# A filter by FFT followed by soft mixture of experts: the softmax chain's steps in another order along the pairs, and the first transform unit of batch 1 behind the first pair

## The chip, the cores and the metric

The kernel runs on one core of a Trainium2 chip. TensorE (PE in the rows) multiplies matrices, VectorE (DVE), ScalarE (ACT) and GpSimd (POOL) work on tiles, and SyncE (SP) issues most DMAs. The metric is device time in microseconds, the median of several executions of the same program; smaller is better.

## The reference

Eight sequences of 2496 rows and 256 channels are filtered in the frequency domain, and the result goes through a soft mixture of 8 experts with 4 slots each. The softmax over the rows (`d`) runs over all 19968 rows of all batches; the one over the slots (`c`) is local to a row.

```python
X = np.fft.rfft(x, axis=1)                      # x: 8 x 2496 x 256
y = np.fft.irfft(X * (filt_r + 1j * filt_i)[None], n=2496, axis=1)
x = y.reshape(19968, 256)
logits = x @ phi                                # 32 slots
d = np.exp(logits - logits.max(0)); d /= d.sum(0) + 1e-09
slot_input = (d.T @ x).reshape(8, 4, 256)
slot_out[e] = np.maximum(slot_input[e] @ w1[e], 0.0) @ w2[e]
c = np.exp(logits - logits.max(1)); c /= c.sum(1) + 1e-09
out = c @ slot_out
```

## The kernel before

**Stages.** A sequence of 2496 rows is transformed in two stages, each a set of small matrix products. Batch 0 is transformed from x directly: `first_stage`, then `turn(c)` transposes a stripe on PE and copies it out (L483, L486). Batches 1 to 7 go in units (b, u), u from 0 to 5: x is loaded, `fold_x` makes sums and differences `sd` and `eo` on DVE and POOL (L378), `s1_unit` multiplies on PE (s, L406), ACT copies the product to `at` (L422), and that goes to DRAM (`a_dram`) and comes back transposed as `ash`. Names such as `s1_1_0` are batch and unit.

**Pairs.** Every batch has five pairs. `x_pair` does the second stage on PE (x, L503) and multiplies by the filter on DVE (t2 at L528, x at L530, the sums y at L531 and L532; from batch 6 the last of them is on POOL). `t_pair` transposes y (PE, L541) and copies it (`yt`, ACT, L547), and `l_unit` makes logits against phi (PE l, L558) and copies them (`lt`, ACT, L569). `x_4_3` is x of batch 4, pair 3. The main loop runs over 80 slots, two to a pair, and a slot also emits the s1 units due in it (`slot_of`).

**Chain.** The batches are grouped as (0,1), (2,3), (4,5), (6,), (7,). Behind each group a generator `chain(g)` brings the logits into the order of time and joins the group to a running softmax: ltr, v1, v, lg (logits; the column maxima `cm` and `cmax` on DVE), mt (transposed maxima, `mx`), mb (spread over partitions, `m_run`), d (DVE L702 subtracts, ACT L710 takes exp), then u, u2 and dd (the inverse steps on PE), z and s (PE sums against y, folded into `s_run` on DVE with the factor `al`, L776 to L781), and `rows()`, the other softmax, in two halves (`rm`, a subtraction, exp, `r_all`). A chain runs while the next batch's pairs run: `hop_slot` takes as many steps of it in slot n as the list `PACE` says. After that the order is a scheduler's, from the order of writing, priorities and the marks `not_before` and `behind`. An engine executes its instructions in that order, so one that waits holds up all behind it.

**End.** The last two chains and the experts' products run after the pairs (about 283 to 331 us), and then the output is formed and written until the end.

Of the kernel before, what the change touches and what calls it, by code (L numbers as in the profile page):

```python
# [86 lines left out]


# [195 lines left out]
def fft_soft_moe(ctx, tc, x0, w0, x, ff, phi, wx, cst, w1q, out):  # L284
# [75 lines left out]
    def fold_x(b, u):  # L360

        lo, hi = PIECE[u]
        w = (hi - lo) * P
        xs = xts.pop((b, u)).rearrange("q k a d -> q (k a d)")[:, 0 : 4 * w].rearrange("q (k a d) -> q k a d", k=2, a=2)
        sd = proda.tile([P, 4 * DIM], F32, tag="sd", name=f"sd{b}_{u}", bufs=DB)
        eo = proda.tile([P, 4 * DIM], F32, tag="eo", name=f"eo{b}_{u}", bufs=EB)
        sd, eo = (
            t[:, 0 : 4 * w].rearrange("q (f a d) -> q f a d", f=2, a=2) for t in (sd, eo)
        )
        early = (b, u) < (1, 2)  # L370
        for k, (o, i0, i1, op) in enumerate((
            (sd[:, 0], xs[:, 0], xs[:, 1], ALU.add),
            (sd[:, 1], xs[:, 0], xs[:, 1], ALU.subtract),
            (eo[:, 0], sd[:, :, 0], sd[:, :, 1], ALU.add),
            (eo[:, 1], sd[:, ::-1, 0], sd[:, ::-1, 1], ALU.subtract),
        )):
# [80 lines left out]
    def first_stage(u):  # L457

        lo, hi = PIECE[u]
        for h in range(lo, hi):  # L460
# [8 lines left out]
            for i in range(2):  # L469
                k = 2 * PK * h + PK * i  # L470
                j = min(PK, N2 - k)
                held[h % 2 + 3] = copy(a0_t[:, :, :, k : k + j], ps[:, i, :, 0:j].rearrange("q g j t -> q t g j"))

    def turn(c):

        if c % 2 == 0:
            ashs[0, c // 2] = prod.tile([P, 4, DIM], F32, tag="ash", name=f"ash0_{c}", bufs=NA)
        ash = ashs[0, c // 2][:, c % 2 * 2 : c % 2 * 2 + 2]
        pt = ps_c.tile([P, 2, 2, P], F32, tag="c", name=f"turn_{c}")
        for k in range(2):  # L480
            for dh in range(2):
                g = a0_t[:, 2 * c + k, 2 * dh : 2 * dh + 2].rearrange("q c k -> q (c k)")
                ins = pe.transpose(pt[:, k, dh, :], g, ident)  # L483
                if c < 2:
                    behind("pe", ins)
        ins = (dve.tensor_copy if c == 1 else act.copy)(ash, pt.rearrange("k p h d -> k p (h d)"))  # L486
        if c == 1:
            held[4] = ins

    def x_pair(b, i):  # L490

# [35 lines left out]
            ys[b, 2 * i + c] = y[:, :, c]  # L527
        dve.tensor_tensor(out=t2, in0=ps[:, ::-1], in1=fiv, op=ALU.mult)  # L528
        add, part = (pool_e, y) if b >= PA else (dve, ps)
        dve.tensor_tensor(out=part, in0=ps, in1=frv, op=ALU.mult)  # L530
        dve.tensor_tensor(out=y[:, 1], in0=part[:, 1], in1=t2[:, 1], op=ALU.add)  # L531
        added[0] = add.tensor_tensor(out=y[:, 0], in0=part[:, 0], in1=t2[:, 0], op=ALU.subtract)  # L532

    def t_pair(b, i):
# [59 lines left out]
    def chain(g):  # L594
# [84 lines left out]
        with tc.high_priority():  # L679
# [72 lines left out]
        for t0 in range(0, HT, TG):  # L752
# [12 lines left out]
            if t0 != 0:  # L765
                yield "dd"

        pz = psum([P, 1], f"z_{g}")
        for b2 in range(nb):
            for j in range(4):  # L770
# [37 lines left out]
        def rows():
            rm = (const if late else wk).tile([KR, NX], F32, tag=f"rm{max(g, NG - 3)}", name=f"rm_{g}", bufs=1)
            rs = r_all[:, g, 0:NX]  # L810
            step = NX // 2
            for x0 in range(0, NX, step):
                sl = slice(x0, x0 + step)
                ins = dve.tensor_reduce(out=rm[:, sl], in_=lgf[:, sl], axis=AX.X, op=ALU.max)
                if x0 == 0 and "sit" in queue:
                    behind("sit", ins)
                if not late:
                    not_before(ins, ended[1])
                    not_before(ins, added[0])
                rmb = rm[:, sl].rearrange("s (x o) -> s x o", o=1).broadcast_to([KR, step, SLOTS])  # L820
                dve.tensor_tensor(out=lgf[:, sl], in0=lgf[:, sl], in1=rmb, op=ALU.subtract)
                ins = act.activation(lgf[:, sl], lgf[:, sl], AF.Exp)
                if not late:
                    not_before(ins, ended[0])
                yield "rows"
                dve.tensor_reduce(out=rs[:, sl], in_=lgf[:, sl], axis=AX.X, op=ALU.add)
                yield "rows"
            dve.tensor_scalar(out=rs, in0=rs, scalar1=1e-9, scalar2=None, op0=ALU.add)
            dve.reciprocal(out=rs, in_=rs)
            if g < NSPILL:  # L830
                c_dram[g] = scr.tile([KR, NH, 2, nb, SLOTS], F32, name=f"c_dram{g}", bufs=1)
                for lo, hi in ((0, CR), (CR, KR)):
                    sp.dma_start(c_dram[g][lo:hi], lg_t[lo:hi])
# [82 lines left out]
    def hop(k=0):  # L916
        if 0 <= k < len(active):
            try:
# [308 lines left out]
```

## Time and profile before

| | us |
|---|---|
| median of the runs (387.44 to 388.2) | 387.52 |
| the profiled execution | 388.1 |
| its span | 386.2 |
| PE busy in it | 332.2 (86%) |
| DVE busy | 277.8 (72%) |
| ACT busy | 190.4 (49%) |
| POOL busy | 181.9 (47%) |

A row of the trace gives the start and the length of a group of like instructions, then engine, line, operation and tiles; the bracket at its end is how long the engine had been idle before it and what released it. Matmul rows count passes, so a number behind x on PE is not a count of lines in the program. PEclk is the share of full clock granted to TensorE, 1.00 being 2.4 GHz and 0.50 being 1.2 GHz.

### The profile page before, as it was taken

What the parts mean: (1) busy time and instruction counts of PE and PEld (TensorE: products, weight loads), DVE (VectorE), ACT (ScalarE), POOL (GpSimd) and SP (SyncE); (2) the same over time, 40 slices, a digit from 0 to 9 for tenths busy, and PEclk for the clock granted to TensorE, in tenths of its full rate; (3) what the DMA queues carried; (4) which work ended last, traced back from release to release, by engine and by line L of the source; (5) the groups of instructions that cost most, each with busy time, mean ns of one, the idle gap of its engine ahead of it and who ended that gap; (6) DMA issues with size and microseconds to landing.
All of it is one profiled execution on the core that took longest, in us unless ns stands there. A gap on an engine that the chain in (4) does not pass through costs nothing.

```text
span 386.2 us, 10001 instructions
## 1 busy us (share of the span) xinstructions
PE 332.2 (86%) x4054; PEld 201.7 (52%) x4054; DVE 277.8 (72%) x406; ACT 190.4 (49%) x393; POOL 181.9 (47%) x178
## 2 busy tenths in 40 slices
PE   8877898889987996987899789799979999989860
PEld 7732343445344543633555444466657635878750
DVE  2489799997896689779928975882976462688540
ACT  2663555546564444662554556365245421676430
POOL 0068978987677465868428581320311302560000
PEclk9999999999998999999699999999989999999655
DMA  8998899899798278979745875951895785499997
GB/s 303 399 378 250 247 279 329 283 341 387 229 319 260 86 208 288 351 204 289 233 122 137 236 215 146 336 161 56 305 347 223 269 290 129 176 415 414 416 415 289
DMA packets 42013, 103.88 MB, mean 269 GB/s; under 512 B 4252, under 2 KB 22556, under 8 KB 39792
## 3 DMA queue, kind: packets, MB, share of 16 engines
q1 hardware_dynamic: 41278, 102.89, 77.8%
q8 instruction: 32, 0.52, 0.5%
q10 hardware_dynamic: 690, 0.36, 0.3%
q14 instruction: 13, 0.11, 0.1%
HBM read 63.11 MB, written 40.12 MB: 267 GB/s over the span
## 4 chain that ended last, share of the span: by engine, by line
PE 52%; DVE 18%; DMA 12%; ACT 7%; issue 4%; POOL 1%; ACTq 0%; DVEq 0%; SPq 0%
PE x L503 8%; PE t L541 7%; PE s L406 7%; DMA out<-ob 5%; PE s L592 5%; ACT at L422 4%; DVE t L528 4%; PE v L592 4%; DMA ff_t<-in_ff 4%; PE u L592 3%; DVE x L530 3%; PE l L558 3%; PE dd L592 3%; DVE d L702 2%; PE out L1177 2%
## 5 line engine op out<-in xcount | busy, mean ns | idle before, releaser
L378 POOL TENSOR_TENSOR eo<-sd 128x512 f32<-128x512 f32 (+1 forms) x80 | 102.2, 1299 | 78.9 <-DVE sd L378 39.2
L528 DVE TENSOR_TENSOR t<-x,ff_t 128x1024 f32<-128x1024 f32 x40 | 48.6, 1215 | 34.2 <-PE x L503 31.9
L547 ACT COPY yt<-t 128x512 f32<-128x512 f32 x80 | 43.6, 588 | 59.9 <-PE t L541 59.8
L503 PE MATMUL x<-ash,cst_t 64*64 64x512 f32 (+3 forms) x352 | 48.9, 583 | 10.0 <-ACT at L422 8.6
L422 ACT COPY at<-s 128x1024 f32<-128x1024 f32 (+1 forms) x42 | 39.5, 941 | 21.4 <-PE s L406 12.9
L406 PE MATMUL s<-eo,w1q_t 64*64 64x512 f32 (+1 forms) x336 | 43.4, 587 | 4.5 <-ACT at L422 4.5
L378 POOL TENSOR_TENSOR sd<-xt 128x512 f32<-128x512 f32 (+1 forms) x36 | 43.9, 1224 | 2.4
L530 DVE TENSOR_TENSOR x<-x,ff_t 128x1024 f32<-128x1024 f32 x30 | 37.0, 1233 | 2.9
L541 PEld LDWEIGHTS t<-cst_t,y 128*128 128x128 f32 x232 | 25.0, 141 | 26.6 <-DVE y L532 10.1
L541 PE MATMUL t<-cst_t,y 128*128 128x128 f32 x232 | 32.8, 280 | 7.0 <-DVE y L532 5.0
L378 DVE TENSOR_TENSOR sd<-xt 128x512 f32<-128x512 f32 (+1 forms) x48 | 37.9, 815 | 0.0
L558 PE MATMUL l<-yt,phi_t 128*32 128x128 f32 x640 | 31.8, 287 | 7.0 <-ACT yt L547 6.8
L1177 PE MATMUL out<-so,st 32*128 32x256 f32 x468 | 35.1, 328 | 2.4 <-ACT ob L1182 1.3
L1177 PEld LDWEIGHTS out<-so,st 32*128 32x128 f32 x468 | 30.1, 214 | 6.7 <-ACT ob L1182 3.5
L532 POOL TENSOR_TENSOR y<-y,t 128x512 f32<-128x512 f32 x9 | 15.0, 1665 | 36.6 <-DVE y L530 31.4
L1182 DVE COPY ob<-out 128x512 f32<-128x512 f32 (+1 forms) x40 | 25.0, 670 | 8.5 <-DMA out<-ob 6.5
L558 PEld LDWEIGHTS l<-yt,phi_t 128*32 128x32 f32 x640 | 17.7, 112 | 22.2 <-ACT yt L547 16.5
L1182 ACT COPY ob<-out 128x512 f32<-128x512 f32 (+1 forms) x40 | 21.7, 582 | 14.8 <-DMA out<-ob 9.0
L503 PEld LDWEIGHTS x<-ash,cst_t 64*64 64x64 f32 (+1 forms) x352 | 12.7, 133 | 24.4 <-ACT at L422 15.3
L592 PE MATMUL s<-y,dd 128*32 128x256 f32 x232 | 19.8, 381 | 0.0
L592 PEld LDWEIGHTS u<-cst_t,d 117*64 117x64 f32 (+3 forms) x440 | 14.9, 139 | 7.0 <-ACT yt L547 2.3
L592 PE MATMUL v<-cst_t,lsb 128*64 128x66 f32 (+1 forms) x400 | 17.4, 235 | 0.0
(127 smaller groups left out, 512.4 us busy)
## 6 DMA issues: line engine op xcount, KB each, us to landing
xt<-in_x SPq DMA_DIRECT2D x35, 512.0 KB
ash<-a_dram SPq DMA_DIRECT2D x35, 512.0 KB
out<-ob SPq DMA_DIRECT2D x17, 1024.0 KB
a_dram<-at SPq DMA_DIRECT2D x70, 240.0 KB
w<-in_wx SPq DMA_DIRECT2D x22, 512.0 KB
x_t<-in_x SPq DMA_DIRECT2D x5, 512.0 KB
ff_t<-in_ff SPq DMA_DIRECT2D x10, 256.0 KB
ff_t<-in_wx SPq DMA_DIRECT2D x5, 512.0 KB
```

What stands on the lines that cost most here:

```text
L378: ins = eng.tensor_tensor(out=o, in0=i0, in1=i1, op=op)
L406: ins = pe.matmul(bf[64 * c : 64 * c + 64, r], w1q_t[q, c], eo[q, c].rearrange("q f d -> q (f d)"), start=True, stop=True,)
L422: copied[0] = act.copy(av, bf.rearrange("q r (f d) -> q f r d", f=2))
L503: ins = pe.matmul(ps[64 * k : 64 * k + 64, r, lo:hi], w[rows], ash[rows, lo:hi, k], start=True, stop=True)
L528: dve.tensor_tensor(out=t2, in0=ps[:, ::-1], in1=fiv, op=ALU.mult)
L530: dve.tensor_tensor(out=part, in0=ps, in1=frv, op=ALU.mult)
L541: ins = pe.transpose(pt[:, dh, r, :], ys[b, 2 * i + c][:, r, dh * P : (dh + 1) * P], ident)
L547: copied[0] = act.copy(yt[:, c], pt)
L558: ins = pe.matmul(pl[32 * j : 32 * j + 32], phi_t[:, dh, :], yt[:, j // 2, dh, :, N2 * (j % 2) : N2 * (j % 2) + N2], start=(dh == 0), stop ...
L592: line(pe.matmul(*a, **k))
L1177: nc.tensor.matmul(prs[k][:, mm, :], sts[n][q, hs, c0 : c0 + P], so[q, ho], start=(i == 0), stop=(i == 2))
L1182: copy(ob[:, nm * k : nm * (k + 1), :], prs[k])
```

## The change

It has four parts.

1. Unit (1,0)'s s1 moves from ahead of the loop into slot 0, behind `x_pair(0, 0)`; the copy of stripe 1 moves from DVE to ACT; and the DVE share of `eo` is kept to unit (1,0) alone.
2. The list `PACE` becomes `PACES`, one list per group. The steps lg4/lg8, mt and mb are drawn into the code of one x pair (`urge`), and the marks order them within its DVE work; u, u2, dd and what follows come earlier in the pairs.
3. `rows()` is a generator of its own, put in the list `side` once dd is done, and advanced in slots in which the chain takes no step.
4. The list of the third group (batches 4 and 5) has no empty slots behind the maxima, so its z and s come earlier too.

```diff
-PACE = (3, 3, 3, 0, 1, 1, 0, 0, 0, 4, 4, 5, 0, 0)
+PACES = ((3, 3, 2, 1, 0, 1, 0, 2, 2, 2, 2) + 4 * (1, 0) + (2,),) * 2 + ((3, 3, 2, 1, 0, 1, 0, 2, 2, 2, 2, 2, 2, 2),)
...
     if b == 1:
-        return u - 1
+        return max(u - 1, 0)
...
-        early = (b, u) < (1, 2)
+        early = (b, u) == (1, 0)
...
-        ins = (dve.tensor_copy if c == 1 else act.copy)(ash, pt.rearrange("k p h d -> k p (h d)"))
+        ins = act.copy(ash, pt.rearrange("k p h d -> k p (h d)"))
         if c == 1:
-            held[4] = ins
+            turned[0] = ins
...
-        dve.tensor_tensor(out=part, in0=ps, in1=frv, op=ALU.mult)
-        dve.tensor_tensor(out=y[:, 1], in0=part[:, 1], in1=t2[:, 1], op=ALU.add)
+        spread = urge("lg8")
+        if spread:
+            held[5] = marks["pe"]
+        ins = dve.tensor_tensor(out=part, in0=ps, in1=frv, op=ALU.mult)
+        if spread:
+            not_before(ins, marks["mx"])
+            urge("mt")
+        ins = dve.tensor_tensor(out=y[:, 1], in0=part[:, 1], in1=t2[:, 1], op=ALU.add)
+        if spread:
+            not_before(ins, marks["m"])
...
-            dve.tensor_reduce(out=mx, in_=pm, axis=AX.X, op=ALU.max)
+            marks["mx"] = dve.tensor_reduce(out=mx, in_=pm, axis=AX.X, op=ALU.max)
...
+        if not late:
+            yield "mb"
...
+        if not late:
+            side.append(rows())
         pz = psum([P, 1], f"z_{g}")
...
-        if g < NG - 2:
-            yield from rows()
-        else:
+        if late:
             late_rows.append(rows())
...
-    for b, u in units[1:]:
+    for b, u in units:
...
     fold_x(1, 0)
-    s1_unit(1, 0)
     sign_tables(0)
...
+    def urge(mark):
+        if active and active[0][0] < NG - 2 and at_mark.get(active[0][0]) == mark:
+            hop()
+            return True
+        return False
...
-        for _ in range(next(steps[active[0][0]], HOPS if active[0][0] == NG - 3 else 1) if paced else HOPS):
+        count = next(steps[active[0][0]], HOPS) if paced else HOPS
+        for _ in range(count):
             if active and active[0][0] < NG - 2:
                 hop()
+        if side and (not paced or count == 0):
+            if next(side[0], None) is None:
+                side.pop(0)
```

**The start, on PE.** Before, the instructions behind stripe 1's turn stand so (`turn_c` is the transposition of stripe c, `s1_1_0` the product of unit (1,0), `x_0_0` the first pair of batch 0; its further pieces are left out of the list by what follows here):

```order
L483 MATMUL turn_2_304<-cst_t_73,a0_t_122 128x128 x4
L483 MATMUL turn_3_328<-cst_t_73,a0_t_122 128x128 x4
L483 MATMUL turn_4_364<-cst_t_73,a0_t_122 128x128 x4
L483 MATMUL turn_5_401<-cst_t_73,a0_t_122 128x128 x4
L483 MATMUL turn_6_440<-cst_t_73,a0_t_122 128x128 x4
L406 MATMUL s1_1_0_244<-eo1_0_238,w1q_t_72 64x256 x4
L483 MATMUL turn_7_478<-cst_t_73,a0_t_122 128x128 x4
L503 MATMUL x_0_0_281<-ash0_0_224,cst_t_73 64x256 x2
```

Now the same engine and place:

```order
L505 MATMUL x_0_0_269<-ash0_0_224,cst_t_73 64x256
L485 MATMUL turn_2_292<-cst_t_73,a0_t_122 128x128 x4
L505 MATMUL x_0_0_269<-ash0_0_224,cst_t_73 64x256
L505 MATMUL x_0_0_269<-ash0_0_224,cst_t_73 64x512
L505 MATMUL x_0_0_269<-ash0_0_224,cst_t_73 64x256 x2
L505 MATMUL x_0_0_269<-ash0_0_224,cst_t_73 64x512
L485 MATMUL turn_3_328<-cst_t_73,a0_t_122 128x128 x4
L406 MATMUL s1_1_0_299<-eo1_0_238,w1q_t_72 64x256 x4
```

The first pair has moved ahead of five turns and of `s1_1_0`.

**The second group's maxima and d, on DVE.** Before, from the last column maximum to `al` (t2, x and the two yb rows are one pair; sd is a unit's fold):

```order
L677 TENSOR_REDUCE cmax_77<-cm_1_1922 117x32
L528 TENSOR_TENSOR t2_4_3_2048<-x_4_3_2043,ff_t_101 128x1024
L530 TENSOR_TENSOR x_4_3_2043<-x_4_3_2043,ff_t_101 128x1024
L531 TENSOR_TENSOR yb_4_2_1982<-x_4_3_2043,t2_4_3_2048 128x512
L532 TENSOR_TENSOR yb_4_2_1982<-x_4_3_2043,t2_4_3_2048 128x512
L378 TENSOR_TENSOR sd6_3_2089<-xt6_3_1797 128x512
L684 TENSOR_REDUCE mx_1_2037<-mt_1_2035 32x1
L528 TENSOR_TENSOR t2_4_4_2110<-x_4_4_2105,ff_t_101 128x1024
L530 TENSOR_TENSOR x_4_4_2105<-x_4_4_2105,ff_t_101 128x1024
L531 TENSOR_TENSOR yb_4_2_1982<-x_4_4_2105,t2_4_4_2110 128x512
L532 TENSOR_TENSOR yb_4_2_1982<-x_4_4_2105,t2_4_4_2110 128x512
L378 TENSOR_TENSOR sd6_4_2141<-xt6_4_1862 128x512
```

(`m_run1`, the three instructions of `d_1` and `al_1` follow there.) Now:

```order
L690 TENSOR_REDUCE cmax_77<-cm_1_1917 117x32
L697 TENSOR_REDUCE mx_1_2048<-mt_1_2046 32x1
L535 TENSOR_TENSOR x_4_3_2039<-x_4_3_2039,ff_t_101 128x1024
L703 TENSOR_TENSOR m_run1_79<-mb_1_2051,m_run0_78 128x32
L539 TENSOR_TENSOR yb_4_2_1968<-x_4_3_2039,t2_4_3_2044 128x512
L542 TENSOR_TENSOR yb_4_2_1968<-x_4_3_2039,t2_4_3_2044 128x512
L378 TENSOR_TENSOR sd6_3_2089<-xt6_3_1792 128x512
L717 TENSOR_TENSOR d_1_2076<-lg_1_1916,m_run1_79 117x512 x2
L717 TENSOR_TENSOR d_1_2076<-lg_1_1916,m_run1_79 117x384
L820 TENSOR_TENSOR al_1_2352<-m_run0_78,m_run1_79 128x32
```

The maxima and `m_run` stand within pair 4_3, d ahead of pair 4_4 instead of behind it; the first and the third group have the same order (the first has no `al`).

**The same place on ACT.** Before:

```order
L547 COPY yt_4_3_2115<-t_4_3_1_2122 128x512
L422 COPY at6_2_2133<-s1_6_2_2128 128x1024
L569 COPY lt_4_1941<-l_4_3_2147 128x128
L547 COPY yt_4_4_2169<-t_4_4_0_2170 128x512
L777 ACTIVATE al_1_2352<-al_1_2352 128x32
```

and now:

```order
L557 COPY yt_4_3_2115<-t_4_3_1_2122 128x512
L821 ACTIVATE al_1_2352<-al_1_2352 128x32
L422 COPY at6_2_2133<-s1_6_2_2128 128x1024
L725 ACTIVATE d_1_2076<-d_1_2076 117x512 x2
```

The exponential of `al_1`, which reads what DVE makes behind `d_1`, has moved ahead of the copy `at6_2`.

In the third group's z and s on PE, all eight z products and 32 of the 40 terms of `s_2` stand ahead of `x_7_2` now; before, all of them stood behind it.

## Rows read from the trace of the kernel before

**Rows 1.** The chain of waits by engine, shares of the span (page, part 4).

```profile
PE 52%; DVE 18%; DMA 12%; ACT 7%; issue 4%; POOL 1%; ACTq 0%; DVEq 0%; SPq 0%
```

**Rows 2.** Windows: length, busy time (instructions) of PE, PEld, DVE, ACT, POOL; PEclk; DMA.

```profile
16.70:32.00 15.30, 12.10 (x84) 6.28 (x83) 13.99 (x21) 9.45 (x18) 7.91 (x6) 1.00 0.94 336
32.00:84.50 52.50, 44.16 (x444) 19.75 (x442) 47.92 (x54) 26.96 (x48) 45.41 (x39) 1.00 0.90 290
84.50:154.50 70.00, 61.93 (x759) 33.20 (x758) 57.58 (x72) 37.88 (x72) 45.51 (x37) 0.98 0.79 259
154.50:226.90 72.40, 63.13 (x759) 34.08 (x760) 58.80 (x74) 37.92 (x74) 46.23 (x37) 0.95 0.74 227
226.90:283.00 56.10, 52.00 (x722) 32.67 (x722) 38.88 (x49) 27.43 (x59) 15.89 (x11) 1.00 0.63 209
```

**Rows 3.** Timeline, the start: start, length, engine, what, and the idle before.

```profile
16.48 0.58 ACT L486 COPY ash<-turn 128x512 f32<-128x512 f32 x1 [0.75 <-PE turn L483]
22.64 1.99 PE L503 MATMUL x<-ash,cst_t 128*64 128x256 f32 x12 [0.92 <-ACT at L422]
28.39 1.01 ACT L422 COPY at<-s 128x1024 f32<-128x1024 f32 x1 [1.29 <-PE s L406]
29.45 1.94 PE L503 MATMUL x<-ash,cst_t 128*64 128x512 f32 x8 [1.12 <-ACT at L422]
```

**Rows 4.** Timeline, first group, from the maxima to pair 3_2.

```profile
96.85 0.69 DVE L663 TENSOR_REDUCE cm<-lg 117x32 f32<-117x512 f32 x1 [0.66 <-PE lg L592]
99.75 0.27 DVE L677 TENSOR_REDUCE cmax<-cm 117x32 f32<-117x96 f32 x1
109.41 3.93 DVE L702 TENSOR_TENSOR d<-lg,m_run 117x512 f32<-117x512 f32 x3
109.41 3.50 POOL L378 TENSOR_TENSOR eo<-sd 128x512 f32<-128x512 f32 x2 [0.69 <-DVE m_run L692]
117.19 1.09 PE L541 MATMUL t<-cst_t,y 128*128 128x128 f32 x8 [2.13 <-DVE y L532]
118.21 1.74 PE L406 MATMUL s<-eo,w1q_t 64*64 64x512 f32 x8
127.39 1.09 PE L503 MATMUL x<-ash,cst_t 64*64 64x512 f32 x8
131.70 0.69 DVE L531 TENSOR_TENSOR y<-x,t 128x512 f32<-128x512 f32 x1 [0.53 <-PE s L592]
```

**Rows 5.** Windows of two stretches, columns as in rows 2.

```profile
118.00:122.00 4.00, 4.00 (x47) 1.99 (x45) 3.86 (x6) 2.02 (x3) 3.64 (x3) 0.57 0.81 267
184.00:188.00 4.00, 3.30 (x28) 1.25 (x30) 4.00 (x7) 3.18 (x7) 0.00 (x0) 0.50 0.43 117
```

**Rows 6.** Timeline, second group, d, al and what waited for them.

```profile
177.62 1.11 PE L503 MATMUL x<-ash,cst_t 64*64 64x256 f32 x12 [0.27 <-ACT at L422]
183.20 0.71 DVE L776 TENSOR_TENSOR al<-m_run,m_run 128x32 f32<-128x32 f32 x1
184.70 1.07 PE L558 MATMUL l<-yt,phi_t 128*32 128x128 f32 x12 [3.58 <-ACT yt L547]
```

**Rows 7.** Timeline, third group: PE's waits, d, the DVE pause, the last transposition.

```profile
243.22 1.12 PE L558 MATMUL l<-yt,phi_t 128*32 128x128 f32 x16 [0.19 <-ACT yt L547]
249.33 2.83 DVE L702 TENSOR_TENSOR d<-lg,m_run 117x512 f32<-117x512 f32 x3
253.05 0.63 PE L558 MATMUL l<-yt,phi_t 128*32 128x128 f32 x12 [0.66 <-ACT yt L547]
267.11 1.23 DVE L528 TENSOR_TENSOR t<-x,ff_t 128x1024 f32<-128x1024 f32 x1 [6.60 <-PE x L503]
281.35 1.21 DVE L530 TENSOR_TENSOR yb_last<-x,ff_t 128x1024 f32<-128x1024 f32 x1
284.53 1.21 PE L541 MATMUL t<-cst_t,yb_last 128*128 128x128 f32 x8 [1.54 <-POOL yb_last L532]
```

**Rows 8.** The chain of waits, a stretch of s in the first group.

```profile
134.53 2.16 PE s L592 x38
```

More of the change, by code (lines that the diff above doesn't have):

```diff
@@ L472, in first_stage @@
                 held[h % 2 + 3] = copy(a0_t[:, :, :, k : k + j], ps[:, i, :, 0:j].rearrange("q g j t -> q t g j"))
+    turned = [None]
     def turn(c):
@@ L578, in fft_soft_moe @@
     chain_end = [None, None]
+    marks = {}
     def line(ins):
+        marks["pe"] = ins
         if floor[0] is not None:
@@ L689, in chain @@
             if g > 0:
-                dve.tensor_tensor(out=m_new, in0=pmb, in1=m_old, op=ALU.max)
+                marks["m"] = dve.tensor_tensor(out=m_new, in0=pmb, in1=m_old, op=ALU.max)
             else:
-                dve.tensor_copy(m_new, pmb)
+                marks["m"] = dve.tensor_copy(m_new, pmb)
+        if not late:
+            yield "mb"
         d = wk.tile([KR, NX, SLOTS], F32, tag="cb", name=f"d_{g}", bufs=1)
@@ L766, in chain, with rows @@
                 yield "dd"
+        def rows():
+            rm = (const if late else wk).tile([KR, NX], F32, tag=f"rm{max(g, NG - 3)}", name=f"rm_{g}", bufs=1)
+            rs = r_all[:, g, 0:NX]
+            step = NX // 2
+            for x0 in range(0, NX, step):
+                sl = slice(x0, x0 + step)
+                ins = dve.tensor_reduce(out=rm[:, sl], in_=lgf[:, sl], axis=AX.X, op=ALU.max)
+                if x0 == 0 and "sit" in queue:
+                    behind("sit", ins)
+                if not late:
+                    not_before(ins, ended[1])
+                    not_before(ins, added[0])
+                rmb = rm[:, sl].rearrange("s (x o) -> s x o", o=1).broadcast_to([KR, step, SLOTS])
+                dve.tensor_tensor(out=lgf[:, sl], in0=lgf[:, sl], in1=rmb, op=ALU.subtract)
+                ins = act.activation(lgf[:, sl], lgf[:, sl], AF.Exp)
+                if not late:
+                    not_before(ins, ended[0])
+                yield "rows"
+                dve.tensor_reduce(out=rs[:, sl], in_=lgf[:, sl], axis=AX.X, op=ALU.add)
+                yield "rows"
+            dve.tensor_scalar(out=rs, in0=rs, scalar1=1e-9, scalar2=None, op0=ALU.add)
+            dve.reciprocal(out=rs, in_=rs)
+            if g < NSPILL:
+                c_dram[g] = scr.tile([KR, NH, 2, nb, SLOTS], F32, name=f"c_dram{g}", bufs=1)
+                for lo, hi in ((0, CR), (CR, KR)):
+                    sp.dma_start(c_dram[g][lo:hi], lg_t[lo:hi])
+        if not late:
+            side.append(rows())
         pz = psum([P, 1], f"z_{g}")
@@ L806, in chain @@
             dve.tensor_copy(s_run[:, 0:DIM], pss)
[L808 to L833, printed above, removed]
-        if g < NG - 2:
-            yield from rows()
-        else:
+        if late:
             late_rows.append(rows())
@@ L845, in sign_tables @@
             fi = ff_t[:, c, 1]
-            act.activation(fi, fi, AF.Copy, scale=C("sgn", c, c + 1))
+            ins = act.activation(fi, fi, AF.Copy, scale=C("sgn", c, c + 1))
+            if c > 1:
+                not_before(ins, turned[0])
     NS = BATCH * CPB
@@ L861, in split_next @@
         for b, u in at_slot.get(n, ()):
-            next_x()
-            fold_x(b, u)
+            if (b, u) != (1, 0):
+                next_x()
+                fold_x(b, u)
     w0_t = ypool.tile([P, 1024], F32, tag="y", name="w0_t")
@@ L928, in run @@
                     at_mark[g] = next(active[k][1])
-    steps = {g: iter(PACE) for g in range(NG - 2)}
+    steps = {g: iter(PACES[g]) for g in range(NG - 2)}
+    side = []
     def hop_slot(n):
@@ L967, in fft_soft_moe @@
     last_s1 = max(at_slot)
-    FREE = (GROUPS[NG - 3][-1] + 1) * CPB + LT - 1 + len(PACE)
+    FREE = (GROUPS[NG - 3][-1] + 1) * CPB + LT - 1 + len(PACES[NG - 3])
     for n in range(NS + LT):
```

## The prediction

> **What bounds the kernel now.** I read the chain of waits first: PE holds 52% of it, DVE 18%, DMA 12% [rows 1]. Next the windows by stage [rows 2]. In the five stretches that the change touches (16.7 to 283 us) PE is busy for 12.10 of 15.30, 44.16 of 52.50, 61.93 of 70.00, 63.13 of 72.40 and 52.00 of 56.10 us: PE is the bound, and what can be won is its idle time and its slow time. The two stretches that hold a whole chain of two batches have a mean granted clock of 0.98 and 0.95, the others 1.00. Third, the timeline where PE waits. At the start it waits for ACT's copies, 0.92 and 1.12 us [rows 3]. In the first group it waits 2.13 us at 117.19 for a y of DVE, since d (3.93 us) lies ahead of that pair on DVE, and right behind this wait an s takes 1.74 us [rows 4] and the window 118 to 122 has a clock of 0.57 [rows 5]: 4.00 x (1 - 0.57) = 1.7 us lost. In the second group it waits 3.58 us for a yt on ACT, which waits behind al, and the window 184 to 188 is all at 0.50 [rows 5, 6]. In the third, DVE pauses for 6.60 us because PE has other work ahead of the x it needs, and PE waits 1.54 us for the last y [rows 7]. Past 283 us (the last chains, experts, output) the instructions are the same but for small moves; I give it 0 +- 0.2.
>
> **The start.** The first pair stood behind five turns and `s1_1_0` and began at 22.64 [rows 3]. It needs stripes 0 and 1 alone, and the first stripe's copy (0.58 us) begins at 16.48, so it can now begin near 17.1, and no longer stands between two units on PE. From there ACT sets the pace. The second x began at 29.45, behind the at copy of 28.39 (1.01 us) [rows 3]. PE's detour for the first x, 1.99 us, is gone from the way to that copy, and one stripe copy of 0.58 comes to ACT from DVE: 1.99 - 0.58 = 1.4 is the most it can give. If one at copy (1.01) is held up by ACT's other work, which is packed closer now, 0.4 is left. I take **-1.0**, nearer to the upper end, because ACT itself was waiting for PE by 1.29 ahead of that copy [rows 3]. Whether it lasts: from 32 to 84.5 PE is busy for 84%, the DMA engines for 0.90 [rows 2]. If transfers set that stretch the gain is gone, end 0. I hold PE and ACT for the bound, since no pair there gets a new wait.
>
> **First group.** I let the new order run with the durations of [rows 4]. cm ends at 96.85 + 0.69 = 97.5. x_2_3 now stands behind the first lg and ends near 97.9 (cm's start and an x of 1.09), t2 (1.23, as in [rows 7]) at 99.1, two more column maxima (0.69 and 0.6) and cmax (0.27) at 100.7; cmax ended at 100.0 before. mt stands directly behind the lg's on PE, so **PE waits some 1.3 us** there, a new wait, with t_2_2, a unit's s and l queued behind. mx is out near 101.3, mb follows t and s (1.09 each), and m_run ends near 103.7. Two y's and a fold (0.69 each) follow, and d begins near 105.7: 3.7 earlier than 109.41. By the order it stands beside eo of POOL as before, so I leave it at 3.93. Pair 2_4 stands behind d on DVE now: 1.23 x 2 + 0.69 x 2 = 3.8, to 113.4, and t_2_4 waits for that, about 1.4 us. Up to x_3_2 the order then has what stood between 117.19 and 127.39 before (t, s, the last of u, l, u2, dd) and, new in it, pair 3_1's x, t and s and one l. The old stretch took 10.2, of which 1.7 went to the clock: 8.5 at full clock, with its short waits for ACT's copies of u in it. x, t and s take 1.09 each, overlapping a little, 3.2 or less, and l about 0.6: 12.2, so x_3_2 begins at 125.6, 1.8 earlier than 127.39. rows() moves its first half into DVE's pause ahead of pair 3_2, which frees some 0.1 of wait later. Sum **-1.9**. Ends: -0.2 if the 1.4 wait brings the low clock as the 2.13 did (1.7), and -2.4 if mt's wait turns out half as long (the cover that it could have is the t behind it).
>
> On d, three instructions took 3.93 beside two eo of POOL, which took 3.50; in the third group, where POOL has no eo, the same three took 2.83 [rows 4, 7]. The Trainium skill, "SBUF — State Buffer", section "Who interferes with whom", says that a DVE instruction with two SBUF inputs contends with a GpSimd instruction that reads SBUF. The rows agree. By that rule moving d pays 1.1 more in each of two groups only if eo is not beside it any longer; by the order it is, and the sum stays.
>
> **Second group.** The same, 70 us later, but for al. d runs from about 175.4 to 179.3, al (0.71 [rows 6]) ends near 180.0. On ACT its exponential stands ahead of the copy `at6_2` now; before, it stood ahead of half of yt_4_4. `at6_2` frees the bank that x_5_0 needs: some 0.25 and 1.01, and x_5_0 begins near 181.2, where it began at 177.62 [rows 6]. PE has only x_5_0 in its row there: **it waits about 3.2 us**, in place of the 3.58 that goes. 3.58 brought the clock to 0.50 [rows 5, 6], so I expect that again. Before, x_5_2 lay 2.1 later against the group's own start than x_3_2 did. Now it has the first group's 1.9 and these 2.1 to win and the late x_5_0 (1.1 to 2.3 beyond the waits that the first group has too) and a slow clock of 1.7 to 2.4 to pay: +1.2 to -0.7 in time. I take **0**.
>
> What goes ahead of the low clock is read from rows here: idle times of 2.13 and 3.58 us [rows 4, 6]; waits of 1.12 and 0.92 at the start left a mean of 1.00 [rows 2, 3]. The new waits of 1.3 to 1.4 lie between. The Trainium skill, "TensorE: Matmul & The Clock Gate", section "Part 1: The HAM clock gate", says that the default state is the throttled one and that activity releases it. The trace agrees so far. By that rule each of the new waits could cost a slow stretch; rival C has what that gives in the first group.
>
> **Third group.** mt waits again, 1.3 us. al's exponential stands ahead of yt_6_3, and l_6_3 waits some 1.4. z and 32 of the 40 terms of s stand ahead of x_7_2: 38 passes took 2.16 [rows 8], so 64 passes and z take 3.8. In exchange u, u2 and dd stand a pair earlier, where PE had six waits of 0.19 to 0.70 between 243.22 and 253.05 [rows 7], 2.6 in all, and 0.5 ahead of lg. 3.8 + 1.3 + 1.4 - 3.1 = 3.4; but the waits partly fall together, and running the order through gives 1.8 at the least. I take 2.6 for t2_7_2 (267.11 before). From there to the end of the last product (281.35 + 1.21) DVE took 15.45; what it has to do by the new order adds up to 14.1, so 1.4 is given back: **+1.2**. Ends +0.2, and +2.9 with a slow stretch (1.7) behind al's wait.
>
> **Sum.** -1.0 - 1.9 + 0 + 1.2 = -1.7 on the profiled execution of 388.1 (a span of 386.2 and 1.9 around it). That is 0.6 above the median of 387.52; the same difference taken from the median gives **385.8**.
>
> **Rivals.**
>
> A, the sum: 385.8, with 384.4 to 386.8 as its own range. For it: d's 3.93 ends up under PE work in the first group, and a PE wait of 2.13 with its slow clock goes. Against it: it rests on a wait of 1.4 being short enough.
>
> B, more: al comes sooner than the 0.71 behind d says [rows 6], for instance because d shrinks where the fold's partner on POOL starts later, the wait behind it is short, and the clock stays at 1.00 in the second group. That gives the first group's 1.9 and 0.7 of the 2.1 besides, 2.6: 383.2.
>
> C, no change: the first group keeps a slow stretch because 1.4 us of wait suffice. -1.0 - 0.2 + 0 + 1.2 = 0: 387.5. The same time comes out if the start gives nothing and the third group loses 0.7 more.
>
> D, slower: al's exponential ahead of a copy, in both later groups. The second pays its upper end (+1.2), the third waits long enough to fall to the low clock (+2.9): -1.0 - 1.9 + 1.2 + 2.9 = +1.2, 388.7. It decides against the change when al's two waits cost more than the 2.9 of the first two parts.
>
> **How the numbers follow.** A 0.40, B 0.16, C 0.24, D 0.20. The range runs from below B to D, without D's far half: 382.9 to 388.7. A measurement of this kernel tells about 0.2%, 0.8 us, from no change: faster is below 386.7, slower above 388.3. A (but for 0.02 above 386.7) and B are faster, 0.54; C and that rest the same, 0.26; D slower, 0.20.
>
> **What would show it.** Right: the second x near 28.0 to 28.5 (wrong: 29 or later); a PE wait of 1 to 1.5 us ahead of mt; d of the first group begun near 105 with eo beside it; x_3_2 near 124.6 (start and group together) and a clock of 1.00 up to it; al on ACT directly ahead of an at copy, then about 3 us of PE wait and a clock of 0.50; t2_7_2 about where it was in spite of 2.9 won ahead of it; a span of 384.5. The forecast is wrong if the start's gain is gone by 84 us, if the clock falls behind the waits of 1.4, or if the third group pays over 2 us for z and s.

## The result, and the profile after

The changed kernel takes 382.71 us (median, 381.44 to 384.06) against 387.48 for the kernel before (four runs, 386.33 to 388.2; the 387.52 of the table ahead is the median of the first three): a ratio of 0.988, 95% interval 0.984 to 0.992, so 4.8 us less (3.0 to 6.2). The forecast was 385.8 with a range from 382.9: the sign is right, the size is not, and the time lies 0.2 below the range. The profiled execution took 382.71 too, with a span of 380.9.

The windows of the profile after, with the cuts of [rows 2], columns as there:

```profile
16.70:32.00 15.30, 13.36 (x92) 6.53 (x92) 15.23 (x15) 10.67 (x21) 11.44 (x8) 1.00 1.01 358
32.00:84.50 52.50, 43.32 (x446) 19.78 (x444) 46.93 (x53) 26.19 (x47) 44.44 (x39) 1.00 0.88 282
84.50:154.50 70.00, 63.76 (x824) 34.82 (x824) 59.31 (x75) 40.12 (x77) 47.19 (x39) 1.00 0.84 278
154.50:226.90 72.40, 63.86 (x787) 35.13 (x778) 58.69 (x74) 38.17 (x75) 47.07 (x37) 0.95 0.72 221
226.90:283.00 56.10, 50.14 (x689) 32.19 (x687) 39.33 (x54) 26.80 (x59) 13.22 (x8) 1.00 0.72 240
```

In the third row PE is busy for 63.76 us where it was 61.93, with 824 instructions instead of 759, at a mean clock of 1.00 instead of 0.98: PE has shorter pauses there, and more work falls into the same stretch. The fourth row still shows 0.95.

The timeline of the profile after, the first group, with the idle time in the bracket as in [rows 4]:

```profile
99.87 0.26 DVE L690 TENSOR_REDUCE cmax<-cm 117x32 f32<-117x96 f32 x1
100.28 0.26 PE L602 MATMUL mt<-cst_t,cmax 117*32 117x117 f32 x1 [1.10 <-DVE cmax L690]
104.71 3.91 DVE L717 TENSOR_TENSOR d<-lg,m_run 117x512 f32<-117x512 f32 x3
104.96 3.25 POOL L378 TENSOR_TENSOR eo<-sd 128x512 f32<-128x512 f32 x2 [4.00 <-DVE sd L378]
112.47 1.09 PE L551 MATMUL t<-cst_t,y 128*128 128x128 f32 x8 [1.43 <-DVE y L542]
113.49 1.09 PE L406 MATMUL s<-eo,w1q_t 64*64 64x512 f32 x8
124.42 1.09 PE L505 MATMUL x<-ash,cst_t 64*64 64x512 f32 x8
```

d begins 4.7 us earlier and is as long as it was; the s behind the wait takes 1.09 us where it took 1.74; the x of pair 3_2 begins 2.97 us earlier. The second group of the same execution, with what answers to [rows 6]:

```profile
174.86 1.24 DVE L820 TENSOR_TENSOR al<-m_run,m_run 128x32 f32<-128x32 f32 x1
176.14 0.23 ACT L821 ACTIVATE al<-al 128x32 f32<-128x32 f32 x1 [3.36 <-DVE al L820]
176.28 1.01 ACT L422 COPY at<-s 128x1024 f32<-128x1024 f32 x1
177.34 2.00 PE L505 MATMUL x<-ash,cst_t 64*64 64x256 f32 x12 [3.70 <-ACT at L422]
179.27 3.67 PE L605 MATMUL u<-cst_t,d 117*64 117x60 f32 x64
```

Here the forecast wait stands: al, its exponential, the copy, then x_5_0 after 3.70 us of idle PE, and behind it an x of 2.00 us (1.11 in [rows 6]) and a u of 3.67 us (2.08 in e5 below), at the lower clock.

To see where the 4.8 us lie, I compare the starts of the same DVE instruction (the t2 of a pair), of the last transposition and of the first output product in each profiled execution with the profiled execution of before (us, negative is earlier). The kernels of the experiments are explained below; the second line is a second execution of the kernel before, the fourth one of the changed kernel.

| kernel | 0_1 | 2_2 | 3_3 | 4_2 | 6_1 | last t | first out |
|---|---|---|---|---|---|---|---|
| before, again (e8) | +0.24 | +1.05 | +1.05 | +1.04 | +0.85 | +0.86 | +0.81 |
| changed | -1.14 | -0.35 | -2.99 | -4.00 | -4.66 | -4.05 | -5.29 |
| changed, again (e10) | -0.97 | -0.59 | -3.22 | -4.23 | -6.11 | -5.48 | -5.24 |
| start alone (e1) | -1.06 | -1.36 | -2.89 | -2.90 | -3.08 | -3.07 | -3.13 |
| changed, old start (e2) | +0.27 | +0.26 | -2.38 | -3.38 | -5.19 | -4.57 | -5.80 |
| exponential of al late (e3) | -1.22 | -1.37 | -4.01 | -5.02 | -7.17 | -7.12 | -6.77 |
| third group held (e4) | -1.25 | -1.35 | -3.99 | -4.99 | -5.78 | -5.24 | -4.10 |
| all of al late (e5) | -0.64 | -0.93 | -3.58 | -4.58 | -9.51 | -9.57 | -10.82 |
| rows beside alone (e6) | +0.47 | +1.62 | +1.62 | +1.39 | +1.41 | +1.19 | +1.19 |
| maxima not within a pair (e7) | -1.30 | -1.62 | -2.03 | -3.04 | -6.17 | -4.34 | -4.00 |
| and d ahead of the fold (e9) | -1.39 | -1.39 | -5.53 | -6.53 | -12.96 | -13.01 | -13.03 |

From column to column: up to 2_2 the start, to 3_3 the first group, to 4_2 the first pairs of batch 4, to 6_1 the second group, to the last t the third, and then the tail. The changed kernel has -0.35, -2.64, -1.01, -0.66, +0.61 and -1.24, its second execution -0.59, -2.63, -1.01, -1.88, +0.63 and +0.24.

### The profile page after: what moved, and what is told of

Read it like the earlier page. It is cut to its first block, busy times and chain, and to the rows that moved or that the text cites. A ratio compares the mean times of both kernels' runs of the same rounds, so it can differ in the third digit from the quotient of the medians.

```text
span 380.9 us, 10014 instructions
## 1 busy us (share of the span) xinstructions
PE 333.0 (87%) x4054; PEld 205.6 (54%) x4054; DVE 278.5 (73%) x403; ACT 191.1 (50%) x394; POOL 182.9 (48%) x180
## 4 chain that ended last, share of the span: by engine, by line
PE 57%; DVE 17%; DMA 10%; ACT 6%; issue 4%; POOL 2%; ACTq 0%; SPq 0%; DVEq 0%; POOLq 0%
PE x L505 8%; PE out L1205 7%; PE t L551 7%; PE s L406 7%; PE s L605 5%; DMA ff_t<-in_ff 4%; DVE t L530 3%; PE u L605 3%; ACT at L422 3%; PE v L605 3%; DMA ash<-a_dram 3%; PE dd L605 3%; DVE d L717 3%; PE l L568 3%; PE h L1149 2%
## 5 line engine op out<-in xcount | busy, mean ns | idle before, releaser
L505 PE MATMUL x<-ash,cst_t 64*64 64x512 f32 (+3 forms) x352 | 50.6, 583 | 12.9 <-ACT at L422 9.4
L378 DVE TENSOR_TENSOR sd<-xt 128x512 f32<-128x512 f32 (+1 forms) x48 | 40.1, 859 | 0.0
L1205 PE MATMUL out<-so,st 32*128 32x256 f32 x468 | 37.2, 379 | 0.7 <-DVE ob L1210 0.6
L1205 PEld LDWEIGHTS out<-so,st 32*128 32x128 f32 x468 | 33.9, 263 | 3.3 <-DVE ob L1210 1.6
L568 PE MATMUL l<-yt,phi_t 128*32 128x128 f32 x640 | 29.3, 279 | 2.4 <-ACT yt L557 2.2
L568 PEld LDWEIGHTS l<-yt,phi_t 128*32 128x32 f32 x640 | 16.3, 109 | 15.8 <-ACT yt L557 10.2
L605 PE MATMUL u<-cst_t,d 117*64 117x60 f32 (+3 forms) x440 | 16.3, 233 | 1.2 <-ACT d L725 1.2
```

Source lines behind the costliest of these rows:

```text
L505: ins = pe.matmul(ps[64 * k : 64 * k + 64, r, lo:hi], w[rows], ash[rows, lo:hi, k], start=True, stop=True)
L568: ins = pe.matmul(pl[32 * j : 32 * j + 32], phi_t[:, dh, :], yt[:, j // 2, dh, :, N2 * (j % 2) : N2 * (j % 2) + N2], start=(dh == 0), stop ...
L605: line(pe.matmul(*a, **k))
L1205: nc.tensor.matmul(prs[k][:, mm, :], sts[n][q, hs, c0 : c0 + P], so[q, ho], start=(i == 0), stop=(i == 2))
```

## The experiments

Each experiment has its own runs of the kernel before beside it; their medians lie between 387.10 and 388.32, and the ratio in brackets, with its 95% interval, is against them.

The theory after the result: the first group gained what the maxima and d bring; the place of al costs most of what the second group could gain in the same way; the rest is the clock of single executions. The rivals are that the start, or the rows list, or the third group's z and s, explain the size.

**e1 and e2: the start alone, and all but the start.** In e1 the diff's lines on the start stand in the kernel before, in e2 they are taken out of the changed kernel. The core of it:

```diff
-        return u - 1
+        return max(u - 1, 0)
...
-        ins = (dve.tensor_copy if c == 1 else act.copy)(ash, pt.rearrange("k p h d -> k p (h d)"))
+        ins = act.copy(ash, pt.rearrange("k p h d -> k p (h d)"))
...
-    s1_unit(1, 0)
```

> The kernel before with the start of the change alone (unit (1,0) behind the first pair, the stripe copy on ACT). Theory T (transfers): the second x comes 1.1 earlier, at 28.3, but by 75 us the pairs wait for ash from DRAM and the lead is gone; total 387.5 +- 0.5, equal to the kernel before. Rival P (the pace of PE and ACT): the lead of 1.1 stays to the end, 386.4.

> The changed kernel with the start as it was. Theory T: nothing is lost by 75 us, total as the changed kernel, 382.7 +- 0.6. Rival P: 1.1 slower, 383.8.

Measured: e1 385.04 us against 387.50 (0.9936, 0.9909 to 0.9963), e2 383.74 (0.9888, 0.9852 to 0.9925). So the start is worth 2.5 us alone and, by the medians, 1.0 on top of the rest. The 1.0 is not shown: e2's interval covers most of the changed kernel's, and in the profiles e2 is 0.5 ahead of it at the first output, since its slow stretch in the second group was shorter. P gave e2's number (383.8), and e1 gained 1.4 more than P said. Theory T has fallen as a rule: in e1 the lead of 1.1 to 1.4 goes on to pair 2_2. In the profile of the changed kernel three x wait for a transfer, and 0.35 of the lead is left at 2_2; timeline, PE:

```profile
62.27 1.09 PE L505 MATMUL x<-ash,cst_t 64*64 64x512 f32 x8 [1.13 <-DMA ash<-a_dram]
72.92 1.09 PE L505 MATMUL x<-ash,cst_t 64*64 64x512 f32 x8 [0.93 <-DMA ash<-a_dram]
78.15 1.11 PE L505 MATMUL x<-ash,cst_t 64*64 64x256 f32 x12 [1.26 <-DMA ash<-a_dram]
```

In the kernel of e5, with the same start, only the last of these waits is there:

```profile
61.69 1.09 PE L505 MATMUL x<-ash,cst_t 64*64 64x512 f32 x8 [0.30 <-ACT at L422]
71.76 1.09 PE L505 MATMUL x<-ash,cst_t 64*64 64x512 f32 x8 [0.34 <-ACT at L422]
76.88 1.11 PE L505 MATMUL x<-ash,cst_t 64*64 64x256 f32 x12 [1.16 <-DMA ash<-a_dram]
```

Whether the lead is lost by the execution or by something in the one program is open: both executions of the changed kernel lost it (e10 below), and e1, e3, e4, e5, e7 and e9 kept 0.9 to 1.6 of it at 2_2.

Why e1's lead grows by 1.5 in the first group, whose chain is untouched there, the timeline of e1 tells:

```profile
115.83 1.09 PE L543 MATMUL t<-cst_t,y 128*128 128x128 f32 x8 [2.12 <-DVE y L534]
116.85 1.09 PE L406 MATMUL s<-eo,w1q_t 64*64 64x512 f32 x8
```

It is the wait of 2.13 us of [rows 4], and the s behind it takes 1.09 and not 1.74: the clock stayed at its upper level (1.00 from 114 to 122 us).

**e8: the kernel before, a second look.** No edit.

> The kernel before, a second profiled execution. If the lower clock behind the waits of 2.13 and 1.54 us comes by itself from the waits, both slow stretches are there again, and the places of all pairs agree within 0.3 us. If it is a matter of the single execution, one or both are missing and the pairs behind are 1.5 earlier.

Measured: 388.81 us, one run. Both slow stretches are there, and the pairs agree within 0.3 us, but for the stretch between 60 and 80 us, where this execution lost 0.8 to transfers. The timeline at the first one:

```profile
118.25 1.18 PE L541 MATMUL t<-cst_t,y 128*128 128x128 f32 x8 [2.14 <-DVE y L532]
119.36 1.99 PE L406 MATMUL s<-eo,w1q_t 64*64 64x512 f32 x8
```

So a wait of 2.1 us brought the low clock in both executions of before and in e6, and not in e1. For the last transposition it is the same: a wait of 1.54 brought it in both executions of before, in e1 and e6, and 1.36 to 1.37 brought it in e3, e7, e9 and e10, not in the first execution of the changed kernel, e2 or e5. In e4 it came there behind a wait of 0.91. So the length of the wait alone does not decide.

**e3 and e5: al out of the way.** In e3 the exponential on ACT, in e5 the subtraction on DVE too, has to wait for the last dd copy:

```diff
-            dve.tensor_tensor(out=al, in0=m_old, in1=m_new, op=ALU.subtract)
+            ins = dve.tensor_tensor(out=al, in0=m_old, in1=m_new, op=ALU.subtract)
+            if not late:
+                not_before(ins, ended[0])
             act.activation(al, al, AF.Exp)
```

> The changed kernel with the exponential of al on ACT behind the last dd copy, so that the at copy and the yt copy no longer stand behind it. Theory W (al's place costs a wait of 3.7 us and a slow clock in the second group, and 1.4 us in the third): the wait ahead of x_5_0 falls to about 0.6, the clock stays at 1.00 there, the second group gains about 2 more and the third up to 1; total 380.0. Rival H: the wait is hidden, since PE has as much to make up later; total 382.7 +- 0.6.

Measured: 380.69 us (0.9813, 0.9782 to 0.9843), 2.0 less than the changed kernel. Theory W holds for the wait (0.60 ahead of x_5_0) and for the total, H is out. The clock was the miss: a new wait stands two steps on, since the subtraction is still ahead of the pair on DVE and is slow there. Timeline of e3:

```profile
173.58 1.47 POOL L378 TENSOR_TENSOR sd<-xt 128x512 f32<-128x512 f32 x1
173.84 1.27 DVE L820 TENSOR_TENSOR al<-m_run,m_run 128x32 f32<-128x32 f32 x1
178.96 1.74 PE L551 MATMUL t<-cst_t,yb 128*128 128x128 f32 x8 [2.62 <-DVE yb L542]
```

An operation on 32 elements a partition lasts 1.27 us beside POOL (0.18 in e7 below, where POOL is idle), and t_4_4 waits 2.62.

> The changed kernel with both the subtraction of al on DVE and its exponential on ACT behind the last dd copy. With the exponential alone moved, the subtraction took 1.27 us ahead of t2_4_4 and t_4_4 waited 2.62 us, with a slow clock behind it. Theory W: that wait becomes the first group's 1.43 us, no slow stretch has to follow, the second group takes as long as the first: 1.2 to 2.9 less than with the exponential alone, 378.5 (377.8 to 379.5). Rival H: the slow stretch comes all the same, and only the 1.2 is won: 379.5.

Measured: 377.36 us against 387.10 (0.9755, 0.9725 to 0.9785), a little better than the lower end expected. The wait is that of the first group now, and what follows runs at the upper clock:

```profile
173.65 1.11 PE L505 MATMUL x<-ash,cst_t 64*64 64x256 f32 x12 [0.60 <-ACT at L422]
174.69 2.08 PE L605 MATMUL u<-cst_t,d 117*64 117x60 f32 x64
178.20 1.09 PE L551 MATMUL t<-cst_t,yb 128*128 128x128 f32 x8 [1.43 <-DVE yb L542]
179.22 1.09 PE L406 MATMUL s<-eo,w1q_t 64*64 64x512 f32 x8
```

The second group gains 4.93 (from 4_2 to 6_1), against 0.66 and 1.88 with al in the way; the third loses nothing (-9.51 to -9.57), against 0.6. So al's place costs the changed kernel about 5 us (5.3 between the medians, 5.0 with each against its own runs of before).

**e4: the third group's z and s behind x_7_2 again.** Three empty slots in its list:

```diff
-... + ((3, 3, 2, 1, 0, 1, 0, 2, 2, 2, 2, 2, 2, 2),)
+... + ((3, 3, 2, 1, 0, 1, 0, 2, 2, 2, 2, 0, 0, 0),)
```

The matmuls are the same 4054 as in the changed kernel. But the list `side` is not run to its end here, and the kernel leaves out the last two DVE instructions of the third group's rows(), the addition of 1e-9 and the reciprocal (0.17 and 0.43 us in the changed kernel). So its output is not that of the reference, and its time is short by up to these 0.6 us.

> The changed kernel with three empty slots in the third group's list, so that z and s stand behind x_7_2 again. Theory S (z and s ahead of x_7_2 cost 2.4 us there, of which DVE's pauses give 1.8 back): t2_7_2 comes 2 earlier, but the last transposition only 0.3 to 1, total 382.2. Rival Z: the 2.4 come back in full: 380.3.

Measured: 384.70 us (0.9930, 0.9895 to 0.9965). t2_7_2 does come earlier, 6.91 ahead of before (the changed kernel 2.22), but the lead falls to 5.24 at the last transposition and to 4.10 at the first output product. Both theories were too kind: what is not done ahead of x_7_2 waits in front of the next steps. DVE's timeline shows one of its pauses for PE, and what comes late:

```profile
271.17 0.69 DVE L668 COPY v<-v 120x512 f32<-120x512 f32 x1 [3.31 <-PE v L602]
279.71 1.67 DVE L789 TENSOR_REDUCE rm<-lg 117x22 f32<-117x704 f32 x2
```

rows()' reductions begin at 279.71, behind the last pair, in the tail. So the early z and s of the change, with the rows() that follow them, are worth about 2 us by the medians (the two intervals touch), and the rival that they cost the 2.4 us is out: 380.3 lies below e4's interval (383.4 to 386.1).

**e6: rows() beside the chain alone, in the kernel before.** rows() moves up into `side` as in the diff, and hop_slot advances it in slots with no step; the list stays PACE.

> The kernel before with rows() as a list beside the chain, and nothing else changed (start, list of steps and maxima as before). Theory R (the side list brings the rows' DVE work into the pause ahead of pair 3_2 and lets the next group's first steps in earlier): 0.9 less in the first group and about 1.1 more in batch 4's pairs 1 and 2; 386.0. Rival M (both come from the maxima's place and the new list): 387.5 +- 0.5.

Measured: 387.22 us against 387.10 (1.0007, 0.9978 to 1.0037). Rival M holds: by itself the side list gives nothing, neither in the first group (+1.62 at 2_2 and at 3_3) nor in batch 4's first pairs (-0.2). The 1.62 arise ahead of both, where a wait of 1.67 us for a transfer at 78.5 us had the lower clock behind it.

**e7: maxima not within a pair.** The changed kernel with `urge` returning at once and the two steps put into the list:

```diff
-        if active and active[0][0] < NG - 2 and at_mark.get(active[0][0]) == mark:
-            hop()
-            return True
         return False
...
-PACES = ((3, 3, 2, 1, 0, 1, 0, ...
+PACES = ((3, 3, 2, 1, 2, 1, 0, ...
```

> The changed kernel with the maxima's steps taken from the list at the end of the slot, so that cm, mx and m_run stand behind the y sums of pair 2_3 and not between its products. Theory O (the order within the pair is what saves time): cmax ends about 2.5 later, PE waits for mx and for m_run one after the other, d begins 2 to 3 later, and each group loses 1.5 to 2.5: 388. Rival D (only the place of d ahead of the next pair counts): 383.2.

Measured: 384.99 us (0.9941, 0.9913 to 0.9970): 2.3 slower than the changed kernel, between the two theories. The timeline of its second group (the first looks the same but for al):

```profile
170.81 0.26 PE L602 MATMUL mt<-cst_t,cmax 117*32 117x117 f32 x1 [1.75 <-DVE cmax L690]
171.83 1.99 PE L505 MATMUL x<-ash,cst_t 64*64 64x512 f32 x8
172.23 2.69 DVE L717 TENSOR_TENSOR d<-lg,m_run 117x512 f32<-117x512 f32 x3
174.85 0.18 DVE L820 TENSOR_TENSOR al<-m_run,m_run 128x32 f32<-128x32 f32 x1
```

mt's wait is 1.75 instead of 1.10 (1.59 instead of 1.16 in the third group), with the lower clock behind it in all three groups. But al comes while POOL is idle, takes 0.18 us on DVE, and only a yt copy stands directly behind its exponential on ACT: the second group gains 3.13 here, where it gained 0.66 and 1.88. The order within the pair wins in the first group (2.64 against 0.41) and in the third, and loses in the second because of al.

**e9: d ahead of the fold.** On top of e5, d is made in the odd slot ahead of the code of the fold, and a fold's DVE instruction may not be issued before d; the first two lists give up the step that this takes (..., 0, 0, 0, ... for ..., 0, 1, 0, ...):

```diff
+            if n % 2 and active and active[0][0] < NG - 3:
+                urge("mb")
             split_next(n + 3)
...
             elif eng is dve and added[0] is not None:
                 not_before(ins, added[0])
+                if "d" in marks:
+                    not_before(ins, marks["d"])
```

> As the kernel with all of al moved, and in the first two groups the fold sd4_3 (and sd6_3) on DVE behind d, so that POOL's eo, which waits for it, no longer runs beside d. Theory C (d takes 3.9 us because POOL holds the second operand's path): d takes 1.9 to 2.8, t2_2_4 begins 1.1 to 1.9 earlier, the wait of 1.43 us ahead of t_2_4 falls to 0.3 or less in both groups, 2 to 3 us in all: 375.0 (374.3 to 376.0). Rival L (d is as long as it is by its own shape, or the wait passes to ACT's exponentials or to eo4_3 for the next unit): 377.4 +- 0.6.

Measured: 375.90 us against 388.32 (0.9693, 0.9646 to 0.9739). Theory C holds. The timeline of its first group:

```profile
103.07 1.75 DVE L719 TENSOR_TENSOR d<-lg,m_run 117x512 f32<-117x512 f32 x3
104.74 0.69 DVE L378 TENSOR_TENSOR sd<-xt 128x512 f32<-128x512 f32 x1
105.60 2.52 POOL L378 TENSOR_TENSOR eo<-sd 128x512 f32<-128x512 f32 x2 [5.68 <-DVE sd L378]
109.93 1.09 PE L553 MATMUL t<-cst_t,y 128*128 128x128 f32 x8
```

d takes 1.75 us for the three instructions that took 3.91, eo 2.52 instead of 3.25, and t_2_4 waits for nothing. Against e5 the first group gains 1.5 more and the second 1.5 (5.53 - 1.39 = 4.14 and 12.96 - 6.53 = 6.43, against 2.65 and 4.93), 3.0 in all; the medians are 1.5 apart, and against their own runs of the kernel before 12.4 and 9.7.

**e10: the changed kernel, a second look.**

> The changed kernel, a second profiled execution. If the lead of the start is lost to transfers each time, t2_2_2 stands 0.4 ahead of the kernel before again; if that was the single execution, 0.9 to 1.4 ahead, as in the other kernels with this start. The lower clock behind x_5_0's wait of 3.7 us is there again; the one behind the last wait of 1.37 us may be there or not.

Measured: 382.76 us. The lead at 2_2 is 0.59: lost to transfers again, though e1, e3, e4, e5, e7 and e9 kept theirs with the same start. The clock behind x_5_0's wait fell again, but rose sooner; timeline:

```profile
177.11 2.00 PE L505 MATMUL x<-ash,cst_t 64*64 64x256 f32 x12 [3.70 <-ACT at L422]
179.04 2.63 PE L605 MATMUL u<-cst_t,d 117*64 117x60 f32 x64
181.60 1.09 PE L551 MATMUL t<-cst_t,yb 128*128 128x128 f32 x8
279.06 1.82 PE L551 MATMUL t<-cst_t,yb_last 128*128 128x128 f32 x8 [1.37 <-POOL yb_last L542]
```

The u took 3.67 in the first execution and 2.63 here; and the last transposition, at the upper clock there, has the lower here. The two differences, 1.22 in the second group and 1.48 in the tail, nearly cancel in the total.

## Why the prediction was wrong, step by step

Four terms of the sum failed. The pairs ahead of the second group's maxima stood in it at nothing, and gave 1.0. The gain that the new order gives a group stood at 1.9, and 2.6 came. The second group was taken as 0, from a sum with its sign turned, and gave 0.7 and 1.9. The third group stood at +1.2 and cost 0.6. The tail's 1.2 in the first profile is chance: the clock of single executions.

**The start, -1.0: right at the second x, 0.35 and 0.59 of it left at 2_2.** The second x began at 28.32 (forecast 28.0 to 28.5). I had asked whether transfers or PE set the stretch up to 84.5 us, and taken one answer; the profiles have both (62.27 and 72.92 us above, against e5). e1's 2.5 us (interval 1.4 to 3.5) are more than its lead of 1.1 to 1.4: in its profile the rest is the slow stretch of the first group that did not come.

**First group, -1.9: the steps right, the gain 0.7 short.** Shifted by the lead of 0.35, cmax ended at 100.5 (forecast 100.7), d began at 105.1 (105.7), t_2_4 at 112.8 (113.4), x_3_2 at 124.8 (125.6); mt waited 1.10 (1.3) and t_2_4 1.43 (1.4), and no slow clock came behind either. Each step was some tenths earlier than my sum of whole durations: neighbours on DVE overlap by about 0.1 (in e9 above d ends at 104.82 and the fold begins at 104.74).

**The pairs ahead of the second group's maxima: a step that I left out, -1.0.** In batch 4 the new list puts ltr and v1 between x_4_1 and t_4_1. The timeline before, PE,

```profile
152.11 1.09 PE L503 MATMUL x<-ash,cst_t 64*64 64x512 f32 x8 [0.56 <-ACT at L422]
153.76 0.66 PE L541 MATMUL t<-cst_t,y 128*128 128x128 f32 x4 [0.56 <-DVE y L532]
154.46 1.04 PE L592 MATMUL v<-cst_t,lsb 128*64 128x66 f32 x28
155.43 0.66 PE L541 MATMUL t<-cst_t,y 128*128 128x128 f32 x4
```

and after:

```profile
149.18 1.09 PE L505 MATMUL x<-ash,cst_t 64*64 64x512 f32 x8 [0.56 <-ACT at L422]
150.46 1.04 PE L605 MATMUL v<-cst_t,lsb 128*64 128x66 f32 x28
151.43 1.09 PE L551 MATMUL t<-cst_t,y 128*128 128x128 f32 x8
```

The wait for y is covered by v1, and t and l run in one piece instead of two. All kernels with the new list have this 1.0 (e2, e3, e4, e5, e7, e9), with or without the maxima in a pair; e1 and e6, with the old one, don't have it.

**Second group, 0: the wait and the price right, the gain short and the sign turned.** PE waited 3.70 (forecast 3.2, with al at 0.71 on DVE; it took 1.24), and the clock was 0.50 (178 to 182 us). The prediction's own terms are 1.9 and 2.1 to win and 2.8 to 4.7 to pay (1.1 to 2.3 for the late x_5_0, 1.7 to 2.4 for the clock). That makes -1.2 to +0.7 in time, and not the "+1.2 to -0.7" that it wrote and that rival D used. What failed is the gain: e5, without al's price, has 4.93 where the text had 4.0. The price came out inside its bounds, 4.93 - 0.66 = 4.27 in the first execution and 4.93 - 1.88 = 3.05 in the second. The rows give its parts. x_5_0 waits 3.10 longer than in e5; x and u take 2.48 longer than in e5 in the first execution and 1.44 in the second; and the 1.43 ahead of t_4_4 goes. The late x_5_0 and the slow clock do come one on top of the other: in the changed kernel DVE had the y for t_4_4 done at 179.83, and PE came to it only at 182.88, behind u:

```profile
179.15 0.68 DVE L542 TENSOR_TENSOR yb<-x,t 128x512 f32<-128x512 f32 x1
182.88 1.26 PE L551 MATMUL t<-cst_t,yb 128*128 128x128 f32 x8
```

**Third group, +1.2: right in its steps, 0.6 too dear.** t2_7_2 lost 2.44 against the pair 6_1 (forecast 2.6) and 1.83 came back by the last transposition (1.4): +0.6. e4 shows that with z and s behind x_7_2 it is no better. The low clock that rival D had behind al's wait in this group did not come: l_6_3 waited 1.36 in both executions, at a clock of 1.00.

**The tail, 0: missed by -1.24 in one execution, by its clock.** The wait ahead of the last transposition is 1.54 before and 1.37 after. In the profiled execution of before some 3 us at the lower clock followed it; in the first of after, none. Windows of the kernel before, then of the first of after:

```profile
286.00:288.00 2.00, 2.00 (x33) 1.62 (x31) 1.33 (x5) 0.69 (x2) 0.00 (x0) 0.50 0.97 385
282.00:286.00 4.00, 2.92 (x71) 2.38 (x66) 2.96 (x11) 2.35 (x7) 0.00 (x0) 1.00 0.83 265
```

e10 has the slow stretch again, with the same total. I had read one execution's clock as the kernel's.

**Sum.** -1.7 was forecast; -4.8 came by the medians, -5.3 and -5.2 at the first output product of the two profiled executions, since the one of before lies 0.6 above its median. Against the forecast the first of them has 1.0 more in the step left out, 0.7 in the first group, 0.7 in the second, 0.6 in the third, 1.2 in the tail, and 0.65 less at the start: 3.6. The second has 1.9 in the second group, 0.2 the other way in the tail and 0.4 less at the start, and comes to the same. That the two agree is luck: the clock gave in the tail of one what it gave in the second group of the other. Rival B, the gain to 383.2, was nearest, though not by its reason: al did not come through quickly. C fell: 1.43 to 1.44 us of wait left the clock up all seven times that it stands in a profile (the changed kernel twice, e2, e3, e4, and e5 in two groups). D fell: al's place costs the second group 3.1 to 4.3, but that comes off the 4.9 that the group gains without it, and the third group kept its clock.

The Trainium skill, "TensorE: Matmul & The Clock Gate", section "Part 1: The HAM clock gate", says that the same kernel comes to the full clock sooner or later from run to run, at its start. Of the way back up within this kernel the two executions of the changed kernel show the like: the same u took 3.67 and 2.63 us behind the same wait. The way down varies here too: 2.12 us of idle PE left the clock at 1.00 in e1, and 2.14 had the lower level behind it in e8.

By the rule of the Trainium skill, "SBUF — State Buffer", section "Who interferes with whom", on which the prediction drew, d should shrink once POOL's eo is not beside it. The trace agrees: in e9 d takes 1.75 us for 3.91. The prediction had put what that is worth at 1.1 (3.93 less 2.83), and it is 2.2.

## What to carry to other kernels

When a chain that hides under other work is moved, follow every instruction it issues to the engine where it queues, the small ones first: here an exponential of 0.23 us on ACT and a subtraction of 32 elements on DVE held back half of the 10 us that the same reordering gives without them (377.4 against 382.7 and 387.1). Look which engine runs beside a slow operation before planning around its duration: d's 3.9 us were 1.75 of its own, and swapping it with the fold ahead of it gave another 1.5 us by the medians (375.9, the best version here). And read a slow stretch behind a wait of 1.4 to 2.1 us as a chance and not as a cost: compare two executions before it enters a sum.

## What the hardware showed beyond that

The same wait of PE has the low clock behind it in some executions and not in others: 2.12 to 2.14 us, three with and one without; 1.36 to 1.37 ahead of the last transposition, four with and three without; but 1.36 to 1.37 ahead of l_6_3, four without; 1.43 to 1.44, seven without; 3.56 to 3.70, eight with. Even where the clock falls, the time until it is back differs: the same u took 3.67 and 2.63 us. The executions of one kernel spread by 1.2 us (e3) to 4.9 (e4), those of the kernel before from 385.6 to 389.9, more than most parts of this change are worth. Some of that is the clock, as the table shows; how much was not measured.
